# Attention and two MLP layers on one core: the last 64 keys of two pairs in one tile, transposes three pairs ahead, fewer loads, and the last layer's weight sums at another rate

## The chip, the cores and the metric

The kernel runs on one core of a Trainium2 chip. Its engines work side by side: TensorE (PE in the profile; PEld are its weight loads), VectorE (DVE), ScalarE (ACT), GpSimd (POOL) and SyncE (SP), whose queue starts most of the DMA transfers. The metric is the device time of one execution in microseconds (us); lower is better.

## The reference, cut to what matters

```python
# q, k, v: (4 batches, 12 heads, 448 positions, 64); cap = 30
scores = cap * tanh((q @ k.T / 8) / cap)
attn   = exp(scores - max) / (sum + 1e-9)
x      = (attn @ v), heads side by side          # (1792, 768)
h = x @ w_in1;  g = h - tanh(h);                 x = g @ w_out1   # 768 -> 2048 -> 768
h = x @ w_in2;  g = h / (1 + exp(-1.702 * h));   out = g @ w_out2
```

Inputs and outputs are float32; the weights arrive as 64-bit floats and are turned into pairs of 32-bit numbers (a high and a low part) on the chip.

## The kernel before, in words

**Attention.** Two heads of a batch form a pair; there are 24 pairs, `g` = 0 to 23, six to a batch. Q and K of a pair are loaded with both heads side by side, and TensorE transposes them (`prep_q`, `prep_k`; lines 352, 361, 362), so that head 0 stands in partitions 0 to 63 and head 1 in 64 to 127. The 448 keys are cut into three chunks of 128 (`c` = 0, 1, 2) and a tail of 64 (`c` = `KC` = 3). Scores are made with the keys in the partitions: for a full chunk two products, one per head, each with 64 contraction rows, 128 output partitions and 448 columns (line 376). For the tail, the 64 keys of head 0 and the 64 keys of head 1 stand in the two diagonal blocks of the tile `kt`, whose other blocks are zero; so one product over all 128 rows (line 372) gives the tail of both heads, 128 x 448. `pair_act` runs Tanh and Exp on ScalarE: 128 x 896 for a full chunk, 128 x 448 for the tail. `pair_pv` multiplies by V: two products per chunk, one per head, each with 64 output partitions (line 409), and one 128 x 128 product for the tail, with V again in diagonal blocks (`vt`, line 406). `key_adds` adds the four Exp tiles on VectorE, the tail in two halves of 64 partitions (line 398); `pair_sum` sums that over the partitions (line 418).

**Order.** The loop over `g` in `attention()` is written out so that the engines overlap, and `pin` keeps that order on each engine. In iteration `g`, TensorE does scores 1 and 2 of `g`, the first V product, `pair_sum(g - 1)`, the transposes of `g + 2`, the tail's V product, the tail scores and scores 0 of `g + 1`, and the last four V products. The score tiles come from a pool of two buffers, and the V products of all pairs share one PSUM bank, which `pair_out` empties. Beside that, nine chunks of weights are converted (`conv_at`), and results of batches 0 and 1 are scaled and split (`split_at`), with the scale rows `wb` loaded from DRAM.

**The MLP layers** run twice, for batches 0 and 1 and then for 2 and 3. Each product is three passes, high x high, high x low and low x high. In the second run the two output products (`gemm_out_seven`, `gemm_rows_seven`) use seven block products instead of eight, which needs sums of weight blocks: `s1` to `s4` in the first layer, `t1` to `t4` in the second. `weight_combos` makes them as a generator of 28 steps for layer 0 and 36 for layer 1: it loads weight blocks, adds them on VectorE, splits them, and writes the sums to DRAM. `ahead(i)` is called once for each chunk of weights in use; it fetches the weights two chunks ahead (`LEAD`) and advances the generator by one step. What is left of it at the end of a `gemm_in` is run there at once.

Of the kernel before, what the change touches and what calls it, by code (L numbers as in the profile page):

```python
# [37 lines left out]
def attention_moe_moe(ctx, tc, q, k, v, cap, w_in1, w_out1, w_in2, w_out2, out):  # L38
# [269 lines left out]

    def load_qk(g, q_from=None, k_from=None):
        if g >= NG:  # L310
            return
        b, hp = divmod(g, NP)
        t = raw_p.tile([P, 2, 2 * C * D], F32, tag="raw", name="raw")
        for j in range(2):
            a = slice(j * D, (j + 1) * D)
            (q_from or nc.sync).dma_start(
                out=t[:CP, 0].rearrange("p (c e) -> p c e", c=C)[:, :, a],
                in_=q[b, 2 * hp + j].rearrange("(p c) d -> p c d", c=C),
            )
        for j in range(2):  # L320
            a = slice(j * D, (j + 1) * D)
            src = k[b, 2 * hp + j]
            k_dma = (k_from or nc.sync).dma_start
            k_dma(
                out=t[:, 1].rearrange("p (c e) -> p c e", c=C)[:, :KC, a],
                in_=src[:KC * P].rearrange("(p c) d -> p c d", c=KC),
            )
# [16 lines left out]
    QK = S + (KC + 1) * P  # L344

    def prep_q(g):
        if g >= NG:
            return
        qkt[g] = st_p.tile([P, QK], F32, tag="qk", name="qk")
        ps = ps_s.tile([P, 512], F32, tag="s", name="ps_qk")  # L350
        for c in range(C):
            pin(nc.tensor.transpose(ps[:, c * CP:(c + 1) * CP], raw[g][:CP, 0, c * P:(c + 1) * P], ident[:CP, :CP]))  # L352
        hi_dve(qkt[g][:, :S], ps[:, :S])

    def prep_k(g):
# [4 lines left out]
        for c in range(KC):  # L360
            pin(nc.tensor.transpose(ps[:, c * P:(c + 1) * P], t[:, 1, c * P:(c + 1) * P], ident))  # L361
        pin(nc.tensor.transpose(ps[:, KC * P:], kt[g % 4], ident))
        (hi_act if g == 0 else hi_dve)(qkt[g][:, S:], ps)

    def scores(g, c):
# [4 lines left out]
        kc = slice(S + c * P, S + (c + 1) * P)  # L370
        if c == KC:
            pin(nc.tensor.matmul(ps[:, 0, :S], qk[:, kc], qk[:, :S], start=True, stop=True))  # L372
        else:
            for j in range(2):
                a = slice(j * D, (j + 1) * D)
                pin(nc.tensor.matmul(ps[:, j, :S], qk[a, kc], qk[a, :S], start=True, stop=True))  # L376
        sc_t[g, c] = ps

    def pair_act(g, cs):
        for c in cs:  # L380
            ps = sc_t.pop((g, c))
            if c == KC:
                t = tt[g, c] = tl_p.tile([P, S], F32, tag="tl", name="tl")
                ps = ps[:, 0, :S]
            else:
                t = tt[g, c] = t_p.tile([P, 2, S], F32, tag="t", name="t")
                ps = ps[:, :, :S]
            pin(nc.scalar.activation(out=t, in_=ps, func=AF.Tanh, scale=tsc))  # L388
        for c in cs:
            ins = pin(nc.scalar.activation(out=tt[g, c], in_=tt[g, c], func=AF.Exp, scale=cpos))  # L390
        return ins

    def key_adds(g):
        ts = ts_t[g] = ts_p.tile([P, 2, S], F32, tag="ts", name="ts")
        pin(nc.vector.tensor_tensor(out=ts, in0=tt[g, 0], in1=tt[g, 1], op=ALU.add))
        for j in range(2):
            a = slice(j * D, (j + 1) * D)
            pin(nc.vector.tensor_tensor(out=ts[a, j], in0=ts[a, j], in1=tt[g, KC][a], op=ALU.add))
        pin(nc.vector.tensor_tensor(out=ts, in0=ts, in1=tt[g, 2], op=ALU.add))

    def pair_pv(g, c):
        if c == 0:
            r_t[g] = ps_v.tile([P, 512], F32, tag="v", name="ps_pv")
        ps = r_t[g]
        if c == KC:
# [46 lines left out]

    conv_at = [3, 5, 7, 9, 11, 13, 15, 17, 20]
    split_at = [10, 11, 12, 15, 16, 19, 17, 18, 20, 21, 21, 22]

    def attention():
# [8 lines left out]

        load_qk(0, None, nc.scalar)
        nc.sync.dma_start(out=capr, in_=cap.partition_broadcast(P))
# [8 lines left out]
        load_v(1)  # L476
        prep_q(0)
        prep_k(0)
        scores(0, KC)
        scores(0, 0)  # L480
        prep_q(1)
        prep_k(1)
        for g in range(NG):
            pair_act(g, (KC, 0))
            if g - 2 in conv_at:
# [11 lines left out]
            pair_pv(g, 0)  # L497
            if g > 0:
                pair_sum(g - 1)
# [10 lines left out]
            if g >= NP and g % NP < 3:  # L510
# [14 lines left out]
            if g == NG - 1:  # L525
                prepare(1)
                hold[0] = True
                for _ in range(12):
                    next(moe_0)
            scores(g + 1, KC)  # L530
            scores(g + 1, 0)
            key_adds(g)
            pair_pv(g, 1)
            pair_pv(g, 2)
            pair_out(g)
        for _ in range(5):
            next(moe_0)
        hold[0] = False
        pair_sum(NG - 1)
        batch_sums(B - 1)  # L540
# [375 lines left out]
    def moe(b0):  # L916
        last = b0 + NB == B
        if last:
            plain[0] = True
            open_plain()  # L920
            side.append(weight_combos(0))
        yield from gemm_in(0)
        if last:
            for _ in side.pop():
                pass
            side.append(weight_combos(1))
        (gemm_out_seven if last else gemm_out)()
        yield from gemm_in(1)
        if last:
# [7 lines left out]
    for _ in range(WARM_UP):  # L937
        nc.tensor.matmul(wps, wz[:, :P], wz, start=True, stop=True)
    for t in kt:
        nc.vector.memset(t, 0.0)  # L940
    for t in vt:
# [51 lines left out]
```

## Time and profile before

| what | us |
|---|---|
| median of 3 runs | 1135.71 (1135.26 to 1135.86) |
| the profiled execution | 1134.45 |
| its span, first to last instruction | 1132.6 |
| PE busy | 1119.7 (99%) |
| DVE busy | 778.1 (69%) |
| ACT busy | 660.5 (58%) |

All numbers from the trace belong to the one profiled execution, whose own time is 1.3 us below the median. TensorE's granted clock is at full speed from end to end. The attention fills the first 219 us; products of the MLP start to be mixed in at its end and then run alone. A float32 product shows as two MATMUL records, one for each of its passes; a transpose and the high and low products of the MLP show as one. A record's length includes filling and draining the array, so it is the distance between starts that tells what a product costs. "[idle before <- X]" is the time in which the engine stood still before the row, and what ended that.

### The profile page before, as it was taken

The numbers are of one execution on the slowest core, as the hardware profiler recorded it, in microseconds if no ns is written. First come the engines' busy times: TensorE is split into PE (matmuls) and PEld (weight loads), VectorE is DVE, ScalarE is ACT, GpSimd is POOL, SyncE is SP. The second block draws the span as 40 slices with busy tenths as digits, with TensorE's granted clock in tenths as the row PEclk, the third lists the DMA queues.
The fourth block names the chain that finished last, engine by engine and source line by source line (L and its number), as shares of the span: only waits on it lengthen the run. The fifth ranks groups of instructions, "written<-read, shape, count | busy, mean of one in ns | idle before, by whom it ended". The sixth has DMA issues, their size and how long they took to land.

```text
span 1132.6 us, 15911 instructions
## 1 busy us (share of the span) xinstructions
PE 1119.7 (99%) x5627; PEld 920.0 (81%) x5627; DVE 778.1 (69%) x1206; ACT 660.5 (58%) x961; POOL 1.8 (0%) x16
## 2 busy tenths in 40 slices
PE   9999999999999999999999999999999999999998
PEld 4444433589889888888999998888998788889998
DVE  4698998799995545777655556999987753455441
ACT  6889998899994535666644436777534332213230
POOL 0000000000000000000000000000000000000000
PEclk9999999999999999999999999999999999999999
DMA  4676776455458776666688887878899985338784
GB/s 108 167 195 181 205 211 210 151 200 191 159 199 283 253 249 224 223 223 217 211 267 264 280 284 257 292 270 295 268 358 343 352 298 189 112 113 289 224 276 144
DMA packets 166878, 261.45 MB, mean 231 GB/s; under 512 B 60512, under 2 KB 101008, under 8 KB 166800
## 3 DMA queue, kind: packets, MB, share of 16 engines
q1 hardware_dynamic: 165280, 259.53, 69.7%
q8 instruction: 44, 0.72, 0.3%
q10 hardware_dynamic: 1520, 0.92, 0.3%
q14 instruction: 34, 0.28, 0.1%
HBM read 173.41 MB, written 86.99 MB: 230 GB/s over the span
## 4 chain that ended last, share of the span: by engine, by line
PE 93%; DVE 3%; DMA 2%; ACT 2%; issue 0%; SPq 0%; DVEq 0%; ACTq 0%
PE ps_h L684 41%; PE ps_o L793 10%; PE ps_y L709 10%; PE ps_o L846 7%; PE ps_y L743 7%; PE ps_sc L376 5%; PE ps_pv L409 5%; PE ps_o L831 1%; PE ps_pv L406 1%; PE ps_sc L372 1%; PE ps_r L418 1%; PE ps_qk L352 1%; DMA wh<-s 1%; PE ps_qk L361 1%; ACT t L388 1%; DVE pair L286 0%
## 5 line engine op out<-in xcount | busy, mean ns | idle before, releaser
L684 PE MATMUL ps_h<-xl,wh 128*128 128x512 f32 (+1 forms) x768 | 280.6, 365 | 0.5 <-DVE xl L82 0.5
L684 PE MATMUL ps_h<-xh,wh 128*128 128x384 f32 (+1 forms) x768 | 279.4, 364 | 0.3 <-DMA wh<-kept 0.3
L684 PE MATMUL ps_h<-xh,wl 128*128 128x512 f32 (+1 forms) x768 | 174.7, 362 | 0.0
L684 PEld LDWEIGHTS ps_h<-xl,wh 128*128 128x128 f32 x768 | 144.2, 188 | 17.5 <-DVE xl L82 0.8
L684 PEld LDWEIGHTS ps_h<-xh,wh 128*128 128x128 f32 x768 | 144.1, 188 | 16.9 <-ACT xh L76 0.6
L684 PEld LDWEIGHTS ps_h<-xh,wl 128*128 128x128 f32 x768 | 139.5, 188 | 16.3 <-issue 1.4
L76 ACT CAST rh<-gr 128x448 fp32r<-128x448 f32 (+1 forms) x80 | 43.2, 540 | 74.5 <-PE ps_o L846 38.5
L607 ACT ACTIVATE g_t<-ps_h 128x512 f32<-128x512 f32 x64 | 35.0, 547 | 87.9 <-PE ps_h L684 87.3
L154 ACT ACTIVATE wr<-wd 128x768 f32<-128x768 f32 x64 | 57.5, 900 | 49.3 <-DVE wl L82 25.3
L82 DVE TENSOR_TENSOR wl<-wr,wh 128x768 fp32r<-128x768 f32 x64 | 61.2, 956 | 31.6 <-ACT wh L76 26.3
L171 DVE SCALAR_TENSOR_TENSOR wr<-wd,wr 128x768 uint32<-128x768 uint32 x64 | 61.3, 958 | 29.4 <-ACT wd L159 28.4
L76 ACT CAST wh<-wr 128x768 fp32r<-128x768 f32 x64 | 53.4, 834 | 46.5 <-PE ps_y L709 24.3
L82 DVE TENSOR_TENSOR rl<-gr,rh 128x448 fp32r<-128x448 f32 (+1 forms) x80 | 46.9, 589 | 42.5 <-ACT rh L76 42.4
L793 PE MATMUL ps_o<-wh,gh 128*128 128x384 f32 x224 | 74.8, 334 | 0.0
L793 PE MATMUL ps_o<-wl,gh 128*128 128x384 f32 x224 | 74.8, 334 | 0.0
L793 PE MATMUL ps_o<-wh,gl 128*128 128x384 f32 x224 | 74.8, 334 | 0.0
L388 ACT ACTIVATE t<-ps_sc,tsc 128x896 f32<-128x896 f32 x72 | 69.9, 1005 | 6.4 <-PE ps_sc L376 5.6
L390 ACT ACTIVATE t<-t,cpos 128x896 f32<-128x896 f32 x72 | 72.0, 1036 | 0.0
L709 PE MATMUL ps_y<-gl,wh 128*128 128x512 f32 (+1 forms) x192 | 69.8, 364 | 0.0
L709 PE MATMUL ps_y<-gh,wh 128*128 128x512 f32 (+1 forms) x192 | 69.7, 363 | 0.0
L376 PE MATMUL ps_sc<-qk 64*128 64x448 f32 x288 | 67.1, 571 | 0.0
L409 PE MATMUL ps_pv<-t,rv 128*64 128x448 f32 x288 | 64.8, 556 | 1.2 <-ACT t L390 0.8
(137 smaller groups left out, 2110.2 us busy)
## 6 DMA issues: line engine op xcount, KB each, us to landing
wh<-kept SPq DMA_DIRECT2D x65, 384.0 KB, 3.9
wl<-kept SPq DMA_DIRECT2D x65, 384.0 KB, 4.0
wd<-in_moe_w_in_dram SPq DMA_DIRECT2D x64, 384.0 KB, 4.1
wd<-in_moe_w_out_dram SPq DMA_DIRECT2D x32, 768.0 KB, 5.4
kept<-wh SPq DMA_DIRECT2D x60, 384.0 KB, 3.4
kept<-wl SPq DMA_DIRECT2D x60, 384.0 KB, 4.2
single<-wr SPq DMA_DIRECT2D x16, 384.0 KB, 6.0
pair<-single SPq DMA_DIRECT2D x16, 384.0 KB, 5.5
```

Of the source, the lines that this page charges most:

```text
L76: pin(nc.scalar.copy(out=dst, in_=src))
L82: pin(nc.vector.tensor_tensor(out=dst, in0=src, in1=hi.bitcast(F32), op=ALU.subtract))
L171: pin(nc.vector.scalar_tensor_tensor(out=u, in0=dbls.pop(i)[:, :, 1], scalar=0x80000007, in1=u, op0=ALU.bitwise_and, op1=ALU.bitwise_or))
L376: pin(nc.tensor.matmul(ps[:, j, :S], qk[a, kc], qk[a, :S], start=True, stop=True))
L388: pin(nc.scalar.activation(out=t, in_=ps, func=AF.Tanh, scale=tsc))
L390: ins = pin(nc.scalar.activation(out=tt[g, c], in_=tt[g, c], func=AF.Exp, scale=cpos))
L409: pin(nc.tensor.matmul(ps[j * D:(j + 1) * D, :S], rawv[g][:, j, c, :], tt[g, c][:, j], start=(c == 0), stop=(c == KC - 1)))
L684: pin(nc.tensor.matmul(ps, w[:, kk, :], x[kk][:, a], start=(m == 0), stop=(m == len(seq) - 1)))
L709: nc.tensor.matmul(bank[e][:, :a1 - a0], w[:, kk, c], x[2 * j + kk][:, a0:a1], start=(j == 0 and m == 0), stop=(j == KF // 2 - 1 and m == ...
L743: nc.tensor.matmul(ps[e], w[:, kk, c], x, start=(k == 0 and m == 0), stop=(k == KH - 1 and m == 2))
L793: nc.tensor.matmul(ps[n][:, :HW], g[2 * j + ff][:, a], w[:, ff, :], start=(j == 0 and m == 0), stop=(j == KF // 2 - 1 and m == len(seq) - 1),)
L846: nc.tensor.matmul(ps[n], x[:, t], w[:, kk, :], start=(k == 0 and m == 0), stop=(k == KH - 1 and m == 2),)
```

## The change: what it does

**The tail of two pairs in one tile.** The tail keys are no longer put in diagonal blocks. They are loaded as one more column block of the raw K tile (64 rows; both heads in one transfer), and transposed with 64 moving columns. For an even pair `g`, `tail_scores(g)` makes the tail of `g` and `g + 1` in one PSUM tile: four products with 64 contraction rows and 64 output partitions each (head by rows, pair by output partitions). Tanh and Exp then run once per two pairs on 128 x 896. The V tail becomes two products per pair with 64 output partitions each, over all 128 rows: `vt` holds the pair's 64 rows of V, and zeros in the other pair's rows. `key_adds` takes the tail in one instruction of 64 x 896.

**Order.** The transposes run three pairs ahead (`st_p` has four buffers) and the loads four; `pair_sum` of two pairs runs in the even iterations; the tail's V product moves behind `key_adds` in the text, next to the other V products; `conv_at` and `split_at` have other numbers.

**Loads.** A pair has five transfers for Q and K instead of six, and two for V instead of three. The first pair's transfers are divided between two queues by head.

**Weight sums.** `ahead` advances the generator by `rate` steps: 1.75 in the two `gemm_in` of the last run, 0.36 in `gemm_out_seven`.

```diff
...
-    st_p = first_pool("stk", 3)
+    st_p = first_pool("stk", 4)
...
-    ts_p = first_pool("tsum", 2)
+    ts_p = first_pool("tsum", 4)
...
-    kt = [one_p.tile([P, P], F32, name=f"kt{i}") for i in range(4)]
-    vt = [one_p.tile([P, P], F32, name=f"vt{i}") for i in range(3)]
+    vt = [one_p.tile([P, P], F32, name=f"vt{i}") for i in range(4)]
...
-    side = []
+    side, due, rate = [], [0.0], [1.0]
...
         if side:
-            next(side[0], None)
+            due[0] += rate[0]
+            while due[0] >= 1:
+                due[0] -= 1
+                next(side[0], None)
...
-            k_dma(out=kt[g % 4][a, a], in_=src[KC * P:])
+        queues[1].dma_start(
+            out=t[:KT, 1, KC * P:].rearrange("p (h d) -> p h d", h=2),
+            in_=k[b, 2 * hp:2 * hp + 2, KC * P:].rearrange("h p d -> p h d"),
+        )
         raw[g] = t
+
+    def tail_rows(g):
+        return slice(g % 2 * KT, (g % 2 + 1) * KT)
...
-        for j in range(2):
-            nc.sync.dma_start(out=vt[g % 3][j * D:(j + 1) * D, j * D:(j + 1) * D], in_=v[b, 2 * hp + j, KC * P:])
+        nc.sync.dma_start(
+            out=vt[g % 4][tail_rows(g)].rearrange("p (h d) -> p h d", h=2),
+            in_=v[b, 2 * hp:2 * hp + 2, KC * P:].rearrange("h p d -> p h d"),
+        )
...
-        pin(nc.tensor.transpose(ps[:, KC * P:], kt[g % 4], ident))
-        (hi_act if g == 0 else hi_dve)(qkt[g][:, S:], ps)
+        pin(nc.tensor.transpose(ps[:, KC * P:S], t[:KT, 1, KC * P:], ident[:KT, :KT]))
+        (hi_act if g == 0 else hi_dve)(qkt[g][:, S:], ps[:, :S])
...
+    def tail_scores(g):
+        if g >= NG:
+            return
+        ps = ps_b.tile([P, 2, 512], F32, tag="b", name="ps_tl")
+        for n in (g, g + 1):
             for j in range(2):
                 a = slice(j * D, (j + 1) * D)
-                pin(nc.tensor.matmul(ps[:, j, :S], qk[a, kc], qk[a, :S], start=True, stop=True))
-        sc_t[g, c] = ps
+                pin(nc.tensor.matmul(
+                    ps[tail_rows(n), j, :S], qkt[n][a, S + KC * P:], qkt[n][a, :S], start=True, stop=True
+                ))
+        sc_t[g, KC] = ps
...
     def key_adds(g):
         ts = ts_t[g] = ts_p.tile([P, 2, S], F32, tag="ts", name="ts")
+        r = tail_rows(g)
         pin(nc.vector.tensor_tensor(out=ts, in0=tt[g, 0], in1=tt[g, 1], op=ALU.add))
-        for j in range(2):
-            a = slice(j * D, (j + 1) * D)
-            pin(nc.vector.tensor_tensor(out=ts[a, j], in0=ts[a, j], in1=tt[g, KC][a], op=ALU.add))
+        pin(nc.vector.tensor_tensor(out=ts[r], in0=ts[r], in1=tail(g)[r], op=ALU.add))
...
-        if c == KC:
-            pin(nc.tensor.matmul(ps[:, :S], vt[g % 3], tt[g, c], start=False, stop=False))
-            return
         for j in range(2):
-            pin(nc.tensor.matmul(
-                ps[j * D:(j + 1) * D, :S], rawv[g][:, j, c, :], tt[g, c][:, j], start=(c == 0), stop=(c == KC - 1)
-            ))
+            a = slice(j * D, (j + 1) * D)
+            w, t = (vt[g % 4][:, a], tail(g)) if c == KC else (rawv[g][:, j, c, :], tt[g, c])
+            pin(nc.tensor.matmul(ps[a, :S], w, t[:, j], start=(c == 0), stop=(c == KC - 1)))
...
-    conv_at = [3, 5, 7, 9, 11, 13, 15, 17, 20]
-    split_at = [10, 11, 12, 15, 16, 19, 17, 18, 20, 21, 21, 22]
+    conv_at = [3, 5, 7, 9, 11, 14, 16, 18, 20]
+    split_at = [10, 11, 12, 14, 15, 21, 16, 17, 18, 21, 22, 22]
...
-        scores(0, KC)
         scores(0, 0)
-        prep_q(1)
-        prep_k(1)
+        prep(1)
+        tail_scores(0)
         for g in range(NG):
-            pair_act(g, (KC, 0))
+            pair_act(g, (0, KC) if g % 2 == 0 else (0,))
...
-            if g > 0:
+            if g % 2 == 0 and g > 0:
+                pair_sum(g - 2)
                 pair_sum(g - 1)
...
-            prep_q(g + 2)
-            prep_k(g + 2)
-            pair_pv(g, KC)
-            load_qk(g + 3)
+            for n in {0: (2,), 1: (3, 4)}.get(g, (g + 3,)):
+                prep(n)
+            for n in {0: (3, 4)}.get(g, (g + 4,)):
+                load_qk(n)
...
-            scores(g + 1, KC)
             scores(g + 1, 0)
+            if g % 2:
+                tail_scores(g + 1)
             key_adds(g)
+            pair_pv(g, KC)
             pair_pv(g, 1)
...
             side.append(weight_combos(0))
+            rate[0] = 1.75
         yield from gemm_in(0)
...
             side.append(weight_combos(1))
+            rate[0] = 0.36
         (gemm_out_seven if last else gemm_out)()
+        rate[0] = 1.75
         yield from gemm_in(1)
```

The first place is TensorE's queue in the attention. Before, this is one iteration, from scores 1 and 2 on; `ps_sc` are score tiles, `ps_pv` V products, `ps_r` the sums, `ps_qk` the transposes:

```order
L376 MATMUL ps_sc<-qk 128x448 x4
L409 MATMUL ps_pv<-t,rv 64x448 x2
L418 MATMUL ps_r<-ts,sel 64x448 x2
L352 MATMUL ps_qk<-ident,raw 128x112 x4
L361 MATMUL ps_qk<-ident,raw 128x128 x3
L362 MATMUL ps_qk<-ident,kt_166 128x128
L406 MATMUL ps_pv<-tl,vt_172 128x448
L372 MATMUL ps_sc<-qk 128x448
L376 MATMUL ps_sc<-qk 128x448 x2
L409 MATMUL ps_pv<-t,rv 64x448 x4
```

Now, an odd iteration, and the start of the even one that follows (`ps_tl` is the tail tile of two pairs):

```order
L380 MATMUL ps_sc<-qk 128x448 x4
L421 MATMUL ps_pv<-t,rv 64x448 x2
L359 MATMUL ps_qk<-ident,raw 128x112 x4
L368 MATMUL ps_qk<-ident,raw 128x128 x3
L369 MATMUL ps_qk<-ident,raw 128x64
L380 MATMUL ps_sc<-qk 128x448 x2
L390 MATMUL ps_tl<-qk 64x448 x4
L421 MATMUL ps_pv<-tl,vt_169 64x448 x2
L421 MATMUL ps_pv<-t,rv 64x448 x4
L380 MATMUL ps_sc<-qk 128x448 x4
L421 MATMUL ps_pv<-t,rv 64x448 x2
L428 MATMUL ps_r<-ts,sel 64x448 x4
```

The tail scores have moved from every iteration to every second one, as four smaller products. The sums stand in the even iterations alone, and the tail's V products have joined the other V products.

The second place is SP's queue in `gemm_out_seven` of the last run, where the products with `s3` and `s1` are fed. `wh` and `wl` are the weights in use, `pair` and `lo` loads of blocks for the second layer's sums, `t` the writes of such sums. Before:

```order
L257 DMA pair<-kept_226 128x768
L258 DMA lo<-kept_226 128x768
L235 DMA wh<-s_1_254 128x768
L235 DMA wl<-s_1_254 128x768
L257 DMA pair<-kept_230 128x768
L258 DMA lo<-kept_230 128x768
L235 DMA wh<-s_2_255 128x768
L235 DMA wl<-s_2_255 128x768
```

Now:

```order
L234 DMA wh<-s_1_251 128x768
L234 DMA wl<-s_1_251 128x768
L267 DMA t_0_262<-pair 128x768
L234 DMA wh<-s_2_252 128x768
L234 DMA wl<-s_2_252 128x768
L259 DMA pair<-kept_219 128x768
L234 DMA wh<-s_3_253 128x768
L234 DMA wl<-s_3_253 128x768
```

Two transfers for the sums stood between two chunks of weights, and one stands there now. Over the 16 chunks of the last four block products it is 28 before and 15 now; over the 16 chunks of the `gemm_in` behind, 20 before and 36 now. The sums of the first layer keep their places.

## Rows read from the trace of the kernel before

**Rows 1.** Whole span: what PE waited for; total us, times, longest us.

```profile
PE ps_sc L372 <- ACT t L388: 2.0, 1, 2.0
PE ps_y L743 <- DMA wh<-s: 1.8, 5, 0.6
PE ps_o L846 <- DMA wh<-t: 1.2, 2, 0.8
...
PE ps_pv L409 <- ACT t L390: 0.8, 1, 0.8
PE ps_sc L372 <- ACT qk L76: 0.7, 1, 0.7
```

**Rows 2.** Windows of 8 and 10 pairs: us; each engine's busy time; clock; DMA.

```profile
27.44:95.01 67.57, 67.57 (x322) 27.34 (x321) 54.86 (x73) 60.38 (x73) 0.00 (x0) 1.00 0.67 181
95.01:179.48 84.47, 84.47 (x403) 34.19 (x401) 79.11 (x110) 79.13 (x99) 0.00 (x0) 1.00 0.68 194
```

**Rows 3.** Timeline of PE over one pair: start us, us, instruction, records.

```profile
128.80 1.77 PE L376 MATMUL ps_sc<-qk 64*128 64x448 f32 x8
130.50 0.97 PE L409 MATMUL ps_pv<-t,rv 128*64 128x448 f32 x4
131.30 0.92 PE L418 MATMUL ps_r<-ts,sel 128*64 128x448 f32 x4
132.16 0.61 PE L352 MATMUL ps_qk<-ident,raw 112*128 112x112 f32 x4
...
132.93 0.27 PE L362 MATMUL ps_qk<-ident,kt 128*128 128x128 f32 x1
133.04 0.92 PE L406 MATMUL ps_pv<-tl,vt 128*128 128x448 f32 x2
133.79 0.92 PE L372 MATMUL ps_sc<-qk 128*128 128x448 f32 x2
134.64 1.02 PE L376 MATMUL ps_sc<-qk 64*128 64x448 f32 x4
135.59 1.72 PE L409 MATMUL ps_pv<-t,rv 128*64 128x448 f32 x8
```

**Rows 4.** The same timeline, cut to moments inside that first group of eight records.

```profile
128.80 0.65 PE L376 MATMUL ps_sc<-qk 64*128 64x448 f32 x2
...
129.28 0.92 PE L376 MATMUL ps_sc<-qk 64*128 64x448 f32 x4
...
130.03 0.54 PE L376 MATMUL ps_sc<-qk 64*128 64x448 f32 x2
```

**Rows 5.** ACT by line, 13 to 222 us: count | busy us, mean ns | idle before.

```profile
L390 ACT ACTIVATE t<-t,cpos 128x896 f32<-128x896 f32 x71 | 71.0, 1036 | 0.0
L388 ACT ACTIVATE t<-ps_sc,tsc 128x896 f32<-128x896 f32 x71 | 68.9, 1005 | 6.0 <-PE ps_sc L376 5.3
L390 ACT ACTIVATE tl<-tl,cpos 128x448 f32<-128x448 f32 x23 | 15.2, 659 | 0.0
L388 ACT ACTIVATE tl<-ps_sc,tsc 128x448 f32<-128x448 f32 x23 | 14.5, 632 | 6.9 <-PE ps_sc L372 6.5
```

**Rows 6.** DVE by line, 13 to 222 us.

```profile
L398 DVE TENSOR_TENSOR ts<-ts,tl 64x448 f32<-64x448 f32 x48 | 29.7, 620 | 1.1
L399 DVE TENSOR_TENSOR ts<-ts,t 128x896 f32<-128x896 f32 x24 | 26.2, 1093 | 2.5
...
L79 DVE COPY qk<-ps_qk 128x512 f32<-128x512 f32 x22 | 15.0, 681 | 0.0
```

**Rows 7.** Timelines of SP and DVE near 190 us.

```profile
189.41 1.11 SPq L446 DMA_DIRECT2D wb<-wrow x2
...
193.12 0.63 DVE L488 TENSOR_TENSOR xs<-xs,wb 128x448 f32<-128x448 f32 x1 [2.87 <-DMA wb<-wrow]
```

**Rows 8.** Windows of the last run: the seven products' end, and the layer behind.

```profile
861.00:906.00 45.00, 43.09 (x198) 35.80 (x196) 31.64 (x49) 15.40 (x27) 0.00 (x0) 1.00 0.98 374
952.00:1012.00 60.00, 60.00 (x298) 53.75 (x297) 25.72 (x50) 12.14 (x26) 0.00 (x0) 1.00 0.35 111
```

More of the change, by code (lines that the diff above doesn't have):

```diff
@@ L307, in attention_moe_moe, with load_qk @@
     tt, tl, sc_t, ts_t, r_t, sum_t, xs = {}, {}, {}, {}, {}, {}, {}
-    def load_qk(g, q_from=None, k_from=None):
+    def load_qk(g, second=None):
         if g >= NG:
@@ L313, in load_qk @@
         t = raw_p.tile([P, 2, 2 * C * D], F32, tag="raw", name="raw")
+        queues = (nc.sync, second or nc.sync)
         for j in range(2):
             a = slice(j * D, (j + 1) * D)
-            (q_from or nc.sync).dma_start(
+            queues[j].dma_start(
                 out=t[:CP, 0].rearrange("p (c e) -> p c e", c=C)[:, :, a],
@@ L321, in load_qk @@
             a = slice(j * D, (j + 1) * D)
-            src = k[b, 2 * hp + j]
-            k_dma = (k_from or nc.sync).dma_start
-            k_dma(
+            queues[j].dma_start(
                 out=t[:, 1].rearrange("p (c e) -> p c e", c=C)[:, :KC, a],
-                in_=src[:KC * P].rearrange("(p c) d -> p c d", c=KC),
+                in_=k[b, 2 * hp + j, :KC * P].rearrange("(p c) d -> p c d", c=KC),
             )
-            k_dma(out=kt[g % 4][a, a], in_=src[KC * P:])
+        queues[1].dma_start(
+            out=t[:KT, 1, KC * P:].rearrange("p (h d) -> p h d", h=2),
+            in_=k[b, 2 * hp:2 * hp + 2, KC * P:].rearrange("h p d -> p h d"),
+        )
         raw[g] = t
+    def tail_rows(g):
+        return slice(g % 2 * KT, (g % 2 + 1) * KT)
     def load_v(g):
@@ L348, in prep_q @@
             return
-        qkt[g] = st_p.tile([P, QK], F32, tag="qk", name="qk")
+        qkt[g] = st_p.tile([P, 2 * S], F32, tag="qk", name="qk")
         ps = ps_s.tile([P, 512], F32, tag="s", name="ps_qk")
@@ L370, in scores @@
         kc = slice(S + c * P, S + (c + 1) * P)
-        if c == KC:
-            pin(nc.tensor.matmul(ps[:, 0, :S], qk[:, kc], qk[:, :S], start=True, stop=True))
-        else:
+        for j in range(2):
+            a = slice(j * D, (j + 1) * D)
+            pin(nc.tensor.matmul(ps[:, j, :S], qk[a, kc], qk[a, :S], start=True, stop=True))
+        sc_t[g, c] = ps
+    def tail_scores(g):
[3 more added lines that the diff above has]
+        for n in (g, g + 1):
             for j in range(2):
                 a = slice(j * D, (j + 1) * D)
-                pin(nc.tensor.matmul(ps[:, j, :S], qk[a, kc], qk[a, :S], start=True, stop=True))
-        sc_t[g, c] = ps
+                pin(nc.tensor.matmul(
+                    ps[tail_rows(n), j, :S], qkt[n][a, S + KC * P:], qkt[n][a, :S], start=True, stop=True
+                ))
+        sc_t[g, KC] = ps
     def pair_act(g, cs):
@@ L381, in pair_act @@
             ps = sc_t.pop((g, c))
[L382 to L388, printed above, removed]
+            t = tt[g, c] = (tl_p if c == KC else t_p).tile([P, 2, S], F32, tag="t", name="tl" if c == KC else "t")
+            pin(nc.scalar.activation(out=t, in_=ps[:, :, :S], func=AF.Tanh, scale=tsc))
         for c in cs:
@@ L391, in pair_act, with tail @@
         return ins
+    def tail(g):
+        return tt[g - g % 2, KC]
     def key_adds(g):
         ts = ts_t[g] = ts_p.tile([P, 2, S], F32, tag="ts", name="ts")
+        r = tail_rows(g)
         pin(nc.vector.tensor_tensor(out=ts, in0=tt[g, 0], in1=tt[g, 1], op=ALU.add))
-        for j in range(2):
-            a = slice(j * D, (j + 1) * D)
-            pin(nc.vector.tensor_tensor(out=ts[a, j], in0=ts[a, j], in1=tt[g, KC][a], op=ALU.add))
+        pin(nc.vector.tensor_tensor(out=ts[r], in0=ts[r], in1=tail(g)[r], op=ALU.add))
         pin(nc.vector.tensor_tensor(out=ts, in0=ts, in1=tt[g, 2], op=ALU.add))
@@ L404, in pair_pv @@
         ps = r_t[g]
[L405 to L407 removed]
         for j in range(2):
[L409 to L411 removed]
+            a = slice(j * D, (j + 1) * D)
+            w, t = (vt[g % 4][:, a], tail(g)) if c == KC else (rawv[g][:, j, c, :], tt[g, c])
+            pin(nc.tensor.matmul(ps[a, :S], w, t[:, j], start=(c == 0), stop=(c == KC - 1)))
     def pair_sum(g):
@@ L464, in x_part @@
             return i, slice(s_ * S, (s_ + 1) * S)
-        load_qk(0, None, nc.scalar)
+        load_qk(0, nc.scalar)
         nc.sync.dma_start(out=capr, in_=cap.partition_broadcast(P))
@@ L476, in attention, with prep @@
         load_v(1)
-        prep_q(0)
-        prep_k(0)
-        scores(0, KC)
+        def prep(g):
+            prep_q(g)
+            prep_k(g)
+        prep(0)
         scores(0, 0)
-        prep_q(1)
-        prep_k(1)
+        prep(1)
+        tail_scores(0)
         for g in range(NG):
-            pair_act(g, (KC, 0))
+            pair_act(g, (0, KC) if g % 2 == 0 else (0,))
             if g - 2 in conv_at:
@@ L538, in attention @@
         hold[0] = False
+        pair_sum(NG - 2)
         pair_sum(NG - 1)
@@ L938, in attention_moe_moe @@
         nc.tensor.matmul(wps, wz[:, :P], wz, start=True, stop=True)
-    for t in kt:
-        nc.vector.memset(t, 0.0)
     for t in vt:
```

1 line of the change is left out of this document (removed).

## The prediction

> **What bounds the kernel now.** I read the page's engine shares first, then what TensorE waited for, then windows of the attention, then TensorE's timeline over one pair, and last the lines of ScalarE, VectorE and the queue of SP. TensorE is busy 99% of the span, and its waits are few: two in the attention for ScalarE, 2.0 and 0.8 us, one of 0.7 at the start, and two in the last run for sums of weights that had not landed, 1.8 and 1.2 [rows 1]. The reader is to see that there is nearly nothing to win by removing waits: a large gain must take work off TensorE. The windows say that the others are close behind. From 95 to 179 us ten pairs take 84.47 us without a gap on TensorE, 8.45 a pair, while VectorE and ScalarE are each busy 79.1, or 94% [rows 2]. So TensorE sets the pace of the attention, and two engines follow with half a microsecond to spare in each pair.
>
> **What a product costs there.** The first group of one pair is four products, eight records. Two records start together at 128.80, two more at 129.28, and the last two at 130.03, with two between [rows 4]. So two products with 64 contraction rows run side by side, first pass beside first pass, second beside second. From 129.28 to 130.03 are two steps, 0.375 us each. The step from 128.80 is 0.10 longer, and the way out is longer too: four steps are 1.50, but the group takes 1.70, to 130.50 [rows 3]. What remains is spent on the change of the array's form, from 64 x 128 to 128 x 64 or back to the whole. I split a pair: 6 steps of full scores, 6 of V (two products side by side), 2 of sums, 2 for the tail's V and 2 for the tail's scores, which use the whole array alone, make 18 steps, 6.75 us; the transposes are 0.88, from 132.16 to 133.04 [rows 3]; of 8.45 there remain 0.82 for five changes of form, 0.16 each. Two pairs are 16.89.
>
> **The change on TensorE.** In two pairs the two tail products of 2 steps go. Four products of 64 x 64 come in. They use different quarters of the array, and two halves overlap in the trace in both directions: by rows in L376, by output partitions in L409, whose four records take 0.80 [rows 3]. No row shows four at once. The bounds: all four side by side, 2 steps; none beside another, 8 steps. I take 2, by the nearest row, L376 with two products, because nothing in rows 4 holds the second product back behind the first one's second pass. The tail's V product becomes two with 64 output partitions, which run side by side in 2 steps, as L409 does; it joins the other V products, so it costs no change of form. The tail's transpose has 64 moving columns instead of 128; 128 take 0.11, from 132.93 to 133.04 [rows 3], so 0.05 less, twice. Changes of form: five in each pair as before, and one more in the odd one, for the quarters. Together 34 steps, 12.75; transposes 1.66; eleven changes, 1.80: 16.21 instead of 16.89. Twelve times 0.68 is 8.2 us less.
>
> The Trainium skill speaks against a part of this: "TensorEngine Tiling (Array Packing)", Key Properties, says that a change of tiling mode drains the engine. The trace agrees, by the 0.20 that the group of 128.80 takes beyond its steps; the rule gives no figure, and by the trace the twelve added changes are 1.9 us, which are in the sum above.
>
> **The other engines.** Are they fast enough for 16.21 in two pairs? ScalarE needed 79.13 in ten pairs, 15.82 in two [rows 2]. Two tail Tanh and two Exp on 448 columns, 2 x (0.632 + 0.659) = 2.58, become one of each on 896, 1.005 + 1.036 = 2.04 [rows 5]: 15.28, or 94%. VectorE needed 15.82. Two adds of half a tail, 0.62 each, become one of 64 x 896. Bounds 0.62 and 1.24, nearest row the 128 x 896 add with 1.09 [rows 6]: 0.15 less a pair. The copy of K has 448 columns instead of 512, which take 0.681 [rows 6]; in proportion 0.07 less. That is 15.38, or 95%. Both keep the reserve that they have now. The moved order gives slack: transposes and their copies are an iteration earlier than needed, and half of the sums too.
>
> SP's queue issues transfers at about 0.55 us each [rows 7]. Two fewer a pair free 1.1 us. That matters near 190 us, where VectorE stood 2.87 us for the scale rows `wb` that SP had issued only at 189.41 [rows 7], and through it ScalarE's next Tanh and TensorE: the 2.0 and probably the 0.8 of rows 1. With less in the queue and the splits moved I expect these 2.8 to go, and 1.0 of new short waits to come where both followers have conversions and splits in the same iterations (bounds 0, and 4.0, some 0.3 in each of twelve): -1.8.
>
> **The start.** TensorE now makes the first tail scores after the transposes of pair 1, and waits until VectorE has copied Q and K, 0.61 (estimated from the 0.681) and 0.68 [rows 6]; before, it went on with scores of pair 0. And the first tail on ScalarE is 2.04 instead of 1.29 [rows 5], before anything is ahead. Nothing hides that. Both in full are 2.0, both hidden 0; I take +1.3. The 0.7 of rows 1 stays.
>
> **The last run.** The waits for `s` blocks, 1.8 in five [rows 1], fall in a stretch where the transfers were at their limit. A chunk of weights is 18 products; 198 in 45.00 us make a chunk 4.1 us [rows 8]. Its weights are 0.79 MB, 192 GB/s, and 28 sum transfers of 0.39 MB over 16 chunks, as the order shows, add 168: 360, beside 374 measured at a share of 0.98 [rows 8]. With 15 over 16 chunks it is 282. These waits should go: -1.8. The transfers move into the second `gemm_in`, where 36 products make a chunk 7.25 us and the load is 111 GB/s [rows 8]; up to four sum transfers a chunk add 217: some 325, below the 374 delivered. VectorE is half idle there, 25.72 of 60.00. So the move costs nothing in its new place, unless a sum that waits in SP's queue holds back weights for more than two chunks. The 1.2 for `t` blocks I leave as it is. Bounds: 0, and -3.0 if both go. The rate of 1.75 in the last run's first `gemm_in` leaves the queue's order as it was: nothing.
>
> **Sum.** -8.2 - 1.8 + 1.3 - 1.8 = -10.5. From the profiled execution's 1134.45 that gives 1123.95. The median of the runs is 1.26 above that execution, so I predict 1125.2. With the bounds of the three small terms the forecast reaches from 1121.7 (no new wait, a free start, both waits of the last run gone) to 1130.7 (4.0 of waits, 2.0 at the start, nothing in the last run).
>
> **Rivals.**
> *The quarters overlap only as halves do.* Each step more than 2 for the tail group costs 12 x 0.375 = 4.5 us. Three steps, one pair of products half over the other: 1129.7. Four, two halves one after the other: 1134.2, where the tail scores cost what they cost now. For it: no row shows more than two at once. Against it: both kinds of halves overlap completely.
> *More than four steps: slower than before.* The place is the tail group in the odd iterations. The point from which it decides is 10.5 / 4.5 = 2.3 steps beyond 2, so above 4.3. Five steps give 1138.7, eight 1152. For it: four streams into the array at once are new. Against it: rows 4, in which a second product does not wait for the passes of the first. By the Trainium skill, "TensorE: Matmul & The Clock Gate", The mechanism, matmuls start and end strictly in program order. If a product's two passes stand next to each other in the queue, that rule would let only a second pass and the next product's first pass run together, five steps for four products: 1138.7. The trace speaks against it for two products, since four products would take five steps there too and rows 4 show four.
> *ScalarE sets the pace.* The even pair now has four tiles of 896 on ScalarE, 4 x 2.04 = 8.2 by the rows' lengths, and with one split of 448 columns (0.6) 8.8, against about 8.4 on TensorE; the odd pair has 6.1. If the two score buffers cannot carry that over, each two pairs lose 0.4: +4.8, 1130.0. For it: only 6% of reserve, and uneven pairs. Against it: ScalarE's reserve did not grow smaller, and 12.9 us of waits for the score tiles show in its own rows today [rows 5], so it runs ahead of TensorE.
>
> **How the numbers follow.** Forecast 66%; ScalarE's pace 13%; overlap as halves 14% (three steps 6, four 8); more than four steps 6% (five 3, more 3); the rest 1%. Less than 0.2% apart, 2.3 us, cannot be told from no change here: 1133.4 to 1138.0. Faster: the forecast, ScalarE's pace and three steps, 85%, with a little off for cases that come together, 84%. The same: mostly four steps, 10%. Slower 6%. The range of 8 in 10 is 1121.5 to 1132: the forecast's own, most of ScalarE's pace, three steps; it leaves out four steps and more, and what is below the best bound.
>
> **What would show it.** Right: the tail group takes about 0.95 us, its eight records starting in two groups of four; two pairs take 16.2 us; TensorE has no wait near 195 us and some short ones elsewhere; the waits for `s` are gone, and the second `gemm_in` shows some 320 GB/s in its middle. Wrong: the tail group at 1.3 us or above; two pairs above 16.6 with ScalarE or VectorE at 98%; new waits for `wh` in the second `gemm_in` or for `t`.

## The result and the profile after

The changed kernel takes 1125.05 us (median of 6 runs, 1124.11 to 1125.74); the kernel before took 1134.89 beside it (1133.37 to 1135.86). The ratio is 0.9913 [0.9900, 0.9925]. The forecast was 1125.2. The time is right to 0.2 us, but two of its four terms were off by about 2.5 us each, in opposite directions, and cancelled. That is what most of this text is about. The profiled execution took 1125.05 too, with a span of 1123.3.

I cut both traces at the same products of TensorE, in us:

| stretch | before | after | difference | forecast |
|---|---|---|---|---|
| start to the first score product | 8.16 | 7.76 | -0.40 | 0 |
| from it to the first product of the first `gemm_out` | 323.19 | 317.73 | -5.46 | -8.7 |
| from there to the first of the seven products | 465.27 | 465.28 | 0 | 0 |
| the seven products | 108.72 | 104.40 | -4.32 | -1.8 |
| second `gemm_in` of the last run, to TensorE's end | 223.46 | 224.23 | +0.77 | 0 |
| together | 1128.80 | 1119.40 | -9.40 | -10.5 |

The first row is no effect of the change: in all traces of this study the first score product started between 6.83 and 8.16, with and without the change.

The second row compares one trace with one trace. The attention of the kernel before ran once more, unchanged, in the run `rate_only` below, and took 325.06 there, 1.9 longer: 1.5 of it in pair 0, where TensorE waits for Q and K of pair 2, and 0.4 in pair 21. So the attention gained 5.5 by this table and 7.3 by that trace.

What TensorE waited for, to be read against [rows 1] (total us, times, longest):

```profile
PE ps_o L863 <- DMA wh<-t: 2.2, 2, 1.6
PE ps_sc L380 <- ACT t L399: 1.8, 2, 1.3
PE ps_pv L421 <- ACT t L399: 1.5, 3, 0.7
...
PE ps_sc L380 <- ACT qk L76: 0.6, 1, 0.6
PE ps_pv L421 <- issue: 0.4, 1, 0.4
PE ps_h L701 <- DMA wh<-kept: 0.3, 1, 0.3
```

The waits for `s` are gone, those for `t` are 2.2 instead of 1.2, and those for ScalarE's Tanh and Exp tiles 3.3 instead of 2.8.

TensorE's timeline over the odd pair that stands where [rows 3] stood (start us, us, instruction, records):

```profile
134.36 1.77 PE L380 MATMUL ps_sc<-qk 64*128 64x448 f32 x8
136.07 0.97 PE L421 MATMUL ps_pv<-t,rv 128*64 128x448 f32 x4
136.97 0.60 PE L359 MATMUL ps_qk<-ident,raw 112*128 112x112 f32 x4
...
137.84 1.07 PE L380 MATMUL ps_sc<-qk 64*128 64x448 f32 x4
138.84 0.98 PE L390 MATMUL ps_tl<-qk 64*64 64x448 f32 x8
```

The same view, cut to two moments inside the tail group, as [rows 4] was:

```profile
138.84 0.61 PE L390 MATMUL ps_tl<-qk 64*64 64x448 f32 x4
...
139.27 0.56 PE L390 MATMUL ps_tl<-qk 64*64 64x448 f32 x4
```

Four records start together and four more 0.43 behind them; the V products follow at 139.76. So the four quarters run side by side and the group takes 0.92.

Windows (us; busy time and instructions of PE, PEld, DVE, ACT, POOL; clock; DMA share; GB/s) of ten undisturbed pairs, of pairs 16 to 22, of the seven products, and of the second `gemm_in`'s first 57 us and next 60:

```profile
45.00:125.97 80.97, 80.97 (x443) 31.07 (x441) 71.97 (x90) 74.14 (x83) 0.00 (x0) 1.00 0.71 201
142.30:201.54 59.24, 56.22 (x292) 20.05 (x292) 52.71 (x68) 54.32 (x64) 0.00 (x0) 1.00 0.72 214
...
790.77:895.17 104.40, 104.32 (x506) 94.44 (x505) 79.67 (x134) 42.45 (x75) 0.00 (x0) 1.00 0.88 295
...
895.17:952.00 56.83, 56.56 (x277) 50.28 (x278) 32.16 (x51) 18.65 (x36) 0.00 (x0) 1.00 0.86 296
952.00:1012.00 60.00, 60.00 (x301) 54.05 (x300) 32.40 (x60) 14.01 (x29) 0.00 (x0) 1.00 0.51 165
```

Ten pairs take 80.97, 16.19 in two. From 142 us on there are 3 us of waits in 59, with ScalarE and VectorE at 92 and 89% on the mean; both had 94% in the ten pairs of [rows 2]. The seven products are nearly without a gap, and the transfers run at 295 GB/s, where the kernel before had 335 over the same stretch (its window stands below, under `rate_only`).

The lines of the followers, for [rows 5, 6]:

```profile
L401 ACT ACTIVATE tl<-tl,cpos 128x896 f32<-128x896 f32 x12 | 12.5, 1045 | 0.0
L399 ACT ACTIVATE tl<-ps_tl,tsc 128x896 f32<-128x896 f32 x11 | 11.1, 1012 | 0.0
...
L76 ACT CAST xh<-xs 128x448 fp32r<-128x448 f32 x12 | 6.7, 572 | 7.8 <-DVE xs L501 7.8
```

```profile
L411 DVE TENSOR_TENSOR ts<-ts,tl 64x896 f32<-64x896 f32 x24 | 26.1, 1086 | 0.8
...
L79 DVE COPY qk<-ps_qk 128x448 f32<-128x448 f32 x44 | 25.3, 614 | 16.6 <-PE ps_qk L359 16.6
```

Tail tiles 2.06 (estimated 2.04), the tail add 1.09 (1.09), the copies 0.61 (0.61): the durations were right. The row that matters is the cast `xh`, the high half of a scaled result: ScalarE stood 7.8 us ahead of it, for VectorE, in five waits. It stood 7.4 there in the kernel before too, in eight waits, the longest of them, 2.9, behind the late scale rows of [rows 7]. VectorE's wait for those rows has gone, as foretold; ScalarE's wait for VectorE has not.

### The profile page after: what moved, and what is told of

Its sections match the earlier page's. It is cut to its first block, busy times and chain, and to the rows that moved or that the text cites. A ratio compares the mean times of both kernels' runs of the same rounds, so it can differ in the third digit from the quotient of the medians.

```text
span 1123.3 us, 15982 instructions
## 1 busy us (share of the span) xinstructions
PE 1110.7 (99%) x5723; PEld 912.6 (81%) x5723; DVE 771.2 (69%) x1178; ACT 653.2 (58%) x937; POOL 2.0 (0%) x17
## 4 chain that ended last, share of the span: by engine, by line
PE 91%; DVE 3%; ACT 3%; DMA 2%; issue 1%; SPq 0%; DVEq 0%
PE ps_h L701 41%; PE ps_o L810 10%; PE ps_y L726 10%; PE ps_y L760 9%; PE ps_o L863 7%; PE ps_pv L421 5%; PE ps_sc L380 3%; PE ps_o L848 1%; PE ps_r L428 1%; ACT t L399 1%; PE ps_qk L359 1%; PE ps_tl L390 1%; DVE qk L79 0%; DVE ts L411 0%; PE ps_qk L368 0%
## 5 line engine op out<-in xcount | busy, mean ns | idle before, releaser
L399 ACT ACTIVATE t<-ps_sc,tsc 128x896 f32<-128x896 f32 x72 | 70.0, 1008 | 11.4 <-PE ps_sc L380 11.2
```

Of the source, the lines that this page charges most:

```text
L399: pin(nc.scalar.activation(out=t, in_=ps[:, :, :S], func=AF.Tanh, scale=tsc))
```

## The experiments

Eleven runs. Each edit is against the changed kernel, but for `rate_only`. "Attention" below is the stretch of the second row of the table; in five traces that leave it as it is, or nearly (after, `attn_only` twice, `store_act`, `tail_order`), it took 317.73 to 317.99, so 0.5 us can be told there from one trace of such a kernel.

**One part alone.** `attn_only` takes the spreading out, `rate_only` puts nothing but it into the kernel before.

```
 attn_only:  -rate[0] = 1.75   -rate[0] = 0.36   +rate[0] = 1.0
 rate_only:  the kernel before, with due and rate as in the change
```

> The changed kernel with the weight sums issued one step a chunk throughout, as in the kernel before, so only the attention differs from it. By the trace of the changed kernel the attention as a whole gained 5.9 us (start of the run's seven products and every stage before it), so 1134.9 - 5.9 = 1129.0, ratio 0.995, and the waits for s blocks are there again (1.8 us by the list of waits). By the prediction's terms (-8.2 - 1.8 + 1.3) it would be 1126.2, ratio 0.992.

> The kernel before with only the weight sums spread (1.75, 0.36 and 1.75 steps a chunk). By the steps from one product's start to the next the seven products lost 4.3 us to late weights before, far more than the 1.8 that the list of waits names; if so 1134.9 - 4.3 = 1130.6, ratio 0.996, or 1131.6 if the longer waits for t blocks (2.2 instead of 1.2 us) come from the later sums. By the prediction's term (-1.8) 1133.1, ratio 0.998. The waits for t tell whether the sums' new place or something else made them longer: 2.2 here if the sums, 1.2 if not.

`attn_only`: 1130.81 (12 runs), ratio 0.9968 [0.9959, 0.9978]. `rate_only`: 1129.27 (5 runs), 0.9950 [0.9937, 0.9962]. So the part of which I expected 1.8 us is worth 4 to 7, and the kernel with the attention's change alone gains only 2.5 to 4.7, less than either sum of its expectation; together 0.8%, about as in the whole change. In the trace of `rate_only` the seven products take 104.39. Both windows of them, before and in `rate_only`:

```profile
796.62:905.34 108.72, 106.56 (x505) 93.45 (x505) 88.91 (x143) 44.85 (x78) 0.00 (x0) 1.00 0.93 335
```

```profile
797.17:901.56 104.39, 104.31 (x506) 94.43 (x505) 78.59 (x131) 42.03 (x74) 0.00 (x0) 1.00 0.87 293
```

With the sums issued as before, the same 504 products are "busy" 106.56, not 104.3. Half of the loss, 2.16, is in gaps; the other 2.2 is in the busy time. TensorE's timeline of the kernel before shows how, at one of the five waits:

```profile
863.99 0.37 PE L743 MATMUL ps_y<-rl,wh 128*128 128x448 f32 x1
864.20 0.36 PE L743 MATMUL ps_y<-rh,wl 128*128 128x448 f32 x1
864.94 0.44 PE L743 MATMUL ps_y<-rh,wh 128*128 128x448 f32 x1 [0.38 <-DMA wh<-s]
865.22 0.36 PE L743 MATMUL ps_y<-rl,wh 128*128 128x448 f32 x1
```

Products start every 0.207 us, but a record lasts 0.36. A wait shows as a gap only where it outlasts the record: from 864.20 to 864.94 are 0.74, 0.54 lost, of which 0.38 are listed; the next step is 0.28, another 0.07. By these two lengths a wait below some 0.15 is not listed at all.

The gain of `attn_only` in its first trace was 5.9, and 3.3 in the median; that run was the fastest of twelve. So it ran once more.

> attn_only once more, for a second trace. There the profiled run was the fastest of twelve (1128.5; median 1130.8), so its trace does not show where the others lost 2.3 us. If late weights in the stretch of the seven products make the difference, this run takes as much longer from the first of the seven products to the next gemm_in than 109.2 us as it is above 1128.5, and the attention ends at 212.5 as there. If it is the attention, 212.5 moves.

1130.69. The first score product comes 1.1 later (8.13, 7.04), the attention behind it is 0.3 shorter, the seven products take 109.83 instead of 109.17, and what follows 224.07 instead of 223.36. So the 2.2 us are not one thing, and neither side of the expectation holds; the seven products make 0.7 of them. In both traces the attention itself is 5.2 and 5.5 shorter than in the kernel before, as in the whole change. What is missing from the time is lost behind it: the seven products took 0.5 and 1.1 longer than the 108.72 before, and in the second trace the rest took 0.6 longer. Why that stretch loses more there is open.

**The quarters.** `tail_halves` puts the tail's V products between the two pairs' quarters, `tail_order` changes their order.

```
 tail_halves:  if g % 2: tail_scores(g+1, n=g+1) ; key_adds(g) ; pair_pv(g, KC) ; if g % 2: tail_scores(g+1, n=g+2)
 tail_order:  -for n in (g, g + 1): for j in range(2):   +for j in range(2): for n in (g, g + 1):
```

> The changed kernel with the four quarter products of two pairs split into two groups of two, with the tail's V products between them, so that no more than two stand side by side. If four at once take the two steps that two take, every two pairs pay two steps more, 0.75 us, and up to two more changes of form, 0.16 each: 12 x 0.75 = 9.0 to 12 x 1.07 = 12.8, so 1134.1 to 1137.9, about the time of the kernel before. If the followers (ScalarE, VectorE) set the pace anyway, less than 4.5 us is lost: under 1129.5.

> The changed kernel with the four quarter products in another order: both pairs' products of the first contraction half, then both of the second. If the quarters are independent, the group again starts in two groups of four records and takes 0.92 us to the next one, and an even and an odd pair take 16.19 together. If what lets products run together is that neighbours in the order differ in their contraction rows, the group takes four steps, 1.7 us, and the time is about 9 us longer.

`tail_halves`: 1133.64 (12 runs), 0.9994 [0.9986, 1.0003], 8.6 us above the change's median, 9.2 by the two ratios, and just below the range expected. Its timeline has the two half groups:

```profile
146.31 0.97 PE L391 MATMUL ps_tl<-qk 64*64 64x448 f32 x4
147.21 0.97 PE L421 MATMUL ps_pv<-tl,vt 128*64 128x448 f32 x4
148.11 0.97 PE L391 MATMUL ps_tl<-qk 64*64 64x448 f32 x4
149.01 1.72 PE L421 MATMUL ps_pv<-t,rv 128*64 128x448 f32 x8
```

Two quarter products take 0.90 to the next group, no less than the 0.92 of all four together. An odd pair takes 8.84 instead of 7.80: 0.75 for two steps, and the 0.29 that is left for two changes of form. Eleven such pairs are 11.4, less some 2.7 of late waits that go when TensorE is slower: the 8.7 by which its attention is longer. So without the overlap of four, nothing of the gain in the attention would be left. `tail_order`, one run: 1124.80; the order makes no difference. Its eight records, too, start as four at 137.99 and four at 138.42:

```profile
137.99 0.98 PE L390 MATMUL ps_tl<-qk 64*64 64x448 f32 x8
138.90 0.97 PE L421 MATMUL ps_pv<-tl,vt 128*64 128x448 f32 x4
```

**The start.**

```
 start_order:  scores(0, 1) ; +if g == 0: tail_scores(0) ; pair_act(0, (1, KC))   ; scores(0, 2) ; pair_act(0, (2,))
```

> The changed kernel with the first tail scores issued behind pair 0's second score products, and ScalarE taking that tile second. The first tail group took 1.76 us at 9.78 where later ones take 0.98, because half of it waits for VectorE's copies of pair 1. If this wait is what the start lost, 0.8 us come back: 1124.3, and iteration 1 starts 0.8 sooner than at 19.06. Rival: ScalarE, 98% busy in that pair, sets the start; then iteration 1 starts within 0.2 us of 19.06 or the gain is gone by iteration 2 (28.81), and the time stays at 1125.0.

1123.30 (4 runs), 0.9908 [0.9891, 0.9925]. From the first score product to iteration 2 there are 19.50 us (7.69 to 27.19), in the changed kernel 21.05: 1.55 come back, twice what I expected, and the attention is 1.55 shorter (316.18). The time alone does not tell this kernel from the change; the trace does. The wait inside the first tail group made ScalarE late as well, which in turn held up the products behind it.

**The late waits.** `split_late` moves ScalarE's cast behind the pair's last Exp, `split_pool` gives it to GpSimd.

```
 split_late:  -hi_act(xh, xs) ahead of scores(g, 1)   +hi_act(xh, xs) behind pair_act(g, (1, 2)) ; lo_dve behind key_adds(g)
 split_pool:  -hi_act(xh, xs)   +nc.gpsimd.tensor_copy(xh, xs) ; lo_dve ahead of key_adds(g)
```

> The changed kernel with ScalarE's half of each x split moved behind the Tanh and Exp of the pair's last two key tiles, and VectorE's half behind the key adds. Theory of the hand-over: ScalarE stood 1.63 us at 153 and 2.12 at 187 because the cast waits for VectorE's product with the scale rows, which stands behind the key adds; with the cast later this idle time goes, and of TensorE's 3.5 us of waits after 140 us at most 1.5 are left: about 1122.5. Rival, ScalarE is simply full (99 to 100% in pairs 12, 16, 18, 19, 22): the waits stay within 0.5 us of 3.5, and the time at 1125.

> The changed kernel with ScalarE's cast of the twelve x splits done by GpSimd (idle in the attention), VectorE's half just ahead of the key adds. The late casts of the run before this one (split_late) took 3.0 us of waits out of pairs 16 to 22 and put back 0.3 in each of five odd pairs and 0.9 in the last. If the loss is ScalarE's (it stands for a hand-over from VectorE, and is full beside), all of TensorE's 3.5 us of waits after 140 us but about 0.5 go and nothing comes back: about 1122.0. Rival: VectorE, at 95 to 98% in the odd pairs, is the one that is late, and GpSimd's casts slow it further: its instructions get longer than 0.62 and 1.09 us, and the time is 1125 or above.

`split_late`: 1124.07 (4 runs), 0.9906 [0.9893, 0.9919]. `split_pool`: 1123.68 (4 runs), 0.9909 [0.9894, 0.9924]. Neither is told apart from the change by its time; the traces tell more. How the wait arises is seen in ScalarE's and VectorE's timelines of the changed kernel:

```profile
150.79 1.04 ACT L401 ACTIVATE t<-t,cpos 128x896 f32<-128x896 f32 x1
153.47 0.57 ACT L76 CAST xh<-xs 128x448 fp32r<-128x448 f32 x1 [1.63 <-DVE xs L501]
```

```profile
150.09 1.08 DVE L411 TENSOR_TENSOR ts<-ts,tl 64x896 f32<-64x896 f32 x1
151.28 1.09 DVE L412 TENSOR_TENSOR ts<-ts,t 128x896 f32<-128x896 f32 x1
152.28 0.62 DVE L79 COPY xs<-ps_pv 128x448 f32<-128x448 f32 x1
152.82 0.61 DVE L501 TENSOR_TENSOR xs<-xs,wb 128x448 f32<-128x448 f32 x1
```

In an odd pair ScalarE has one tile, 2 us, between the Exp that releases VectorE's key adds and the cast; VectorE has three adds, a copy and the product, 4.5 us, ahead of what the cast needs. So ScalarE stands 1.6 us and its next Tanh are late. In the even pairs 16 and 18 it is the other way round: the cast stands behind two Tanh, two Exp and a conversion's cast, VectorE waits 1.16 for it, and its copy of the pair's output comes late. TensorE's next V product, which writes the same PSUM buffer, starts 0.10 behind the end of that copy: the one below ends at 170.33, and the one of 152.28, shown above, at 152.90. So that copy, and not the releaser in brackets, fits the start of both products (VectorE's and TensorE's timelines):

```profile
163.39 0.62 DVE L82 TENSOR_TENSOR xl<-xs,xh 128x448 fp32r<-128x448 f32 x1 [1.16 <-ACT xh L76]
...
169.71 0.62 DVE L79 COPY xs<-ps_pv 128x448 f32<-128x448 f32 x1
```

```profile
153.00 0.97 PE L421 MATMUL ps_pv<-t,rv 128*64 128x448 f32 x4 [0.39 <-issue]
...
170.43 0.97 PE L421 MATMUL ps_pv<-t,rv 128*64 128x448 f32 x4 [0.65 <-ACT t L399]
```

With the cast moved, pairs 16 to 22 take 56.19 in `split_late` instead of 59.24, and 55.19 would be without any wait:

```profile
143.07:199.26 56.19, 55.33 (x295) 20.51 (x293) 51.31 (x67) 52.40 (x62) 0.00 (x0) 1.00 0.73 216
```

But both kernels lose 0.3 in each of five odd pairs, 11 to 19, of which 11 and 13 had lost nothing before: VectorE's half of the split now stands ahead of the copy that empties the V products' PSUM buffer; and `split_late` waits 1.31 in the last pair. GpSimd's cast took 1.0 us, and VectorE's longer instructions rose beside it on the mean (`wl` 0.97 to 1.14, the shift-and-or 0.96 to 1.09; in `best_pool` below only the second rose).

**The waits for `t`.**

```
 store_act:  -q = nc.scalar if last and half and a > n * P else nc.sync   +q = nc.scalar if last and (a > n * P if half else n < 3) else nc.sync
```

> The changed kernel with the first output stores of the last products issued from ScalarE's queue instead of SP's. In the trace eight stores take SP's queue from 1057.06 to 1061.50, ahead of the loads of t blocks that TensorE then waits for, 1.6 and 0.1 us. If the stores make those waits, the first goes and of 2.2 us for t at most 0.7 is left: 1123.4. If the later sums of the changed kernel make them, they stay at 2.2 and the time at 1125.0.

1123.23 (4 runs), 0.9906 [0.9892, 0.9921], as expected, though again not told apart from the change by the time alone. In SP's queue of the changed kernel the stores stand ahead of the load that TensorE waits for:

```profile
1054.11 0.38 SPq L234 DMA_DIRECT2D wh<-t  x1
1057.06 4.44 SPq L922 DMA_DIRECT2D out_dram<-o  x8
1061.61 0.37 SPq L234 DMA_DIRECT2D wh<-t  x1
```

With six of them on ScalarE's queue the waits for `t` are 0.3 in all. The wait of 1.6 is gone in all three kernels that have this edit; in the ten traces without it, `rate_only` and `attn_only` among them, it is there with 0.4 to 1.6. So the stores make it, and the spreading does not. A second wait, 27 us later, ranges from nothing to 1.7 over all traces, with the edit and without; its cause is open.

**Together.** Both have the edits of `start_order` and `store_act`, and

```
 best_late:  if g % 2: hi_act(xh, xs) behind pair_act(g, (1, 2)) ; lo_dve behind pair_out(g)     (even pairs as they were)
 best_pool:  -hi_act(xh, xs)   +nc.gpsimd.tensor_copy(xh, xs)     (lo_dve where it was)
```

> The changed kernel with three things together: the first tail scores behind the second score products (start_order, 1.6 us in its trace), the first stores on ScalarE's queue (store_act, 1.8), and in the odd pairs alone ScalarE's cast behind the last Exp and VectorE's half behind the pair's output copy. In split_late VectorE's half stood ahead of that copy, and five odd pairs lost 0.3 each, as if the next product found the output's PSUM buffer not free. If that is so, these 0.3 are gone, the 3.0 of late waits mostly too, and the time is 1125.05 - 1.6 - 1.8 - 2.5 = 1119.2. If ScalarE's fullness in the even pairs makes the late waits after all, they come back in part: 1121 to 1122.

> As best_late, but the cast on GpSimd in its old place, and VectorE's half in its old place too. GpSimd's cast took 1.0 us instead of 0.57, so VectorE waits for it some 0.4 us longer where it has no conversion to do meanwhile. By the theory of the hand-over the late waits are gone here too, without the 0.3 of the odd pairs: 1119.2. If VectorE is what is late in the odd pairs, they stay or grow: 1121 or above.

`best_late`: 1119.69 (4 runs), 0.9874 [0.9858, 0.9891]. `best_pool`: 1119.09 (4 runs), 0.9868 [0.9853, 0.9883]. Both beat the change; which is the better can't be told. The odd pairs 11 to 17 are back at 7.80 (pair 19 at 7.95 and 7.92), so the place of VectorE's half was the cause of the 0.3. Their attention takes 313.64 and 313.85, about 4 us less than the change's: 1.3 and 1.0 up to iteration 2, and 2.7 and 2.9 of late waits behind it. In `best_pool`, pairs 16 to 22:

```profile
140.54:196.71 56.17, 55.26 (x294) 20.59 (x292) 53.53 (x68) 51.20 (x56) 6.61 (x7) 1.00 0.75 225
```

## Why the prediction was right, and where it was not

- **The products, -8.2: right.** Two pairs take 16.19 (16.21 foretold), 0.70 less than 16.89: -8.4 in twelve. The tail group takes two steps and 0.92 (0.95). `tail_halves` agrees with the step (0.375) and the change of form (0.15 each). The rivals with three or more steps fall: four records start together, 0.43 us ahead of the other four, and the group is over in 0.92. I read the first four as one of each product; the records do not name it. The Trainium skill, "TensorE: Matmul & The Clock Gate", The mechanism, has matmuls start and end strictly in program order. If the two passes of a product stand next to each other in the queue, these traces disagree, as rows 4 already did for two products; how the passes stand there no run shows.
- **The start, +1.3: nearer 2.0 here.** That is what the products (-8.4) and the waits (+0.9, next point) leave of the attention's -5.5, and it was the prediction's upper bound; `start_order` gives 1.55 of it back. The reason was the one given, and the wait inside the first tail group carried on into ScalarE. But the size hangs on one trace of the kernel before: that stretch, from the first score product to iteration 2, took 19.28 there and 1.5 longer in `rate_only`, against which the start would cost some 0.5.
- **The attention's waits, -1.8: wrong, about +0.9.** The step that failed is "I expect these 2.8 to go, and 1.0 of new short waits to come". Counted as delay against an undisturbed pair, the waits of the kernel before come to 3.7 (0.17 in pair 20, 2.43 in 21, 0.86 in 22, 0.27 at the end), those of the change to 4.6 (1.97 in pairs 15 to 20, 1.38 in 21, 0.82 in 22, 0.42 at the end). By the list of waits alone it is 3.2 and 3.5. VectorE's wait for the scale rows went, as foretold, but TensorE kept 2.6 in the last three pairs and got 2.0 of new waits, not 1.0. I looked at the busy shares, and they were as foretold or lower: 92% for ScalarE, 89% for VectorE. What I didn't look at is the order in which the two hand work to each other: the cast that VectorE feeds stands ahead of ScalarE's Tanh, and the odd pairs, with a tile less, leave 2 us to cover 4.5; in the even pairs VectorE stands for the cast. `split_late` and the two last kernels show it by what goes when the cast moves.
- **ScalarE sets the pace, 1130.0: fell as a rival,** since undisturbed even pairs took 8.39, TensorE's own time, with four tiles on ScalarE. That it is nearly full where casts and conversions meet is true (8.51 busy of 8.54 in pair 16), but taking the cast off it (`best_pool`) brought no more than moving it (`best_late`). Of the 12.9 us that the prediction read as waits for the score tiles, the rows name 11.8 as such.
- **The last run, -1.8: the mechanism right, the size wrong, -4.3.** I took the list of waits for the loss. The first row of [rows 8] had the rest: 198 products at 0.207 are 41.0 us and the stretch is 45.0; 4.0 are lost there, and the list has only the 1.9 by which busy time falls short. The transfers in their new place cost nothing in this trace: the second `gemm_in` takes 116.91 where it took 117.15, and has no gap from 897 us to its end, with 296 GB/s in its first 57 us (341 in the fullest 20, from 930 to 950, where at most 325 was foretold). But a sign named for being wrong, new waits for `wh` in the second `gemm_in`, did come in other kernels with the spreading: six of ten traces wait 0.8 to 1.6 for the third product of that layer, and the layer then takes 117.5 to 118.1 (119.8 with the fall of the clock told below); the three traces without the spreading have 117.15 to 117.30. The +0.8 from there to TensorE's end is not settled either: with the spreading and the stores left on SP's queue that stretch took 223.74 to 226.50 in seven traces, and without the spreading 223.36 to 224.06 in three.
- **From the execution to the median, +1.26.** I added the distance of the earlier median from its profiled execution; beside the change that distance was 0.44. Without it the forecast would have been 1123.95, 1.1 too low: the stretches came out +3.2, -2.5, +0.8 and -0.4 from their terms, and the 1.26 happened to cover the rest.

## What to carry to other kernels

To see what late data cost a stretch, multiply its products by the step between two undisturbed ones and subtract that from its length; gaps and the list of waits show only what outlasts a record, here half. Where two engines follow a third at some 92%, follow one item through both of them in their program order before calling it free: an engine that waits for another ahead of its main work loses time at any mean share. And a sum that comes out right proves its terms no more than a wrong one: measure each where it stands.

## What was not expected of the hardware

In the trace of `split_pool`, TensorE waited 1.55 us for weights after the seven products, was busy 1.07 of 2.70 us, and then ran 3.5 us at a granted clock of 0.53, the lower of its two levels (1.2 GHz); there a step took 0.427 instead of 0.213, 1.7 us lost on top of the wait. In `best_late` a wait of 1.49 at the same place was followed by no such fall.

```profile
892.50:895.20 2.70, 1.07 (x5) 0.31 (x4) 2.65 (x5) 1.54 (x3) 0.00 (x0) 1.00 0.86 329
895.20:896.00 0.80, 0.80 (x4) 0.69 (x5) 0.00 (x0) 0.00 (x0) 0.00 (x0) 0.93 1.12 403
896.00:899.50 3.50, 3.50 (x10) 2.81 (x9) 0.00 (x0) 0.00 (x0) 0.00 (x0) 0.53 1.00 383
```

The 64 x 896 add took 1.086, as long as the 128 x 896 one, 1.092: with half the partitions it is no faster.
